# Setting a planner's durations, its rule for two shared engines and its due times anew, in a kernel of attention and two gated MLPs

## The chip, the cores and the metric

The kernel runs on one core of a Trainium2 chip. A core has five engines that run side by side: TensorE (PE, the matmuls), VectorE (DVE), ScalarE (ACT), GpSimd (POOL) and SyncE (SP), which here issues the transfers. The metric is the device time of one launch in microseconds; three runs of the kernel before gave 1060.21 us as the median (1059.39 to 1060.55).

## The reference

```python
# q, k, v: 4 batches x 8 heads x 576 positions x 64
scores = q @ k.T / 8                     # masked: heads 0-3 a window of 32 positions,
attn = softmax(masked scores)            # heads 4-7 every 4th of the last 128 positions
x = heads side by side of (attn @ v)     # 2304 tokens x 512
xn = x / sqrt(mean(x*x) + 1e-6) * rms_g
g = xn @ w_gate;  h = silu(g) * (xn @ w_val);  x = h @ w_out      # 512 -> 1536 -> 512
gate = sigmoid(x @ w_gate2)
return (gate * (x @ w_val2)) @ w_out2                             # 512 -> 1536 -> 512
```

The six weights come as 64-bit numbers and are turned into f32 on the chip.

## The kernel before, in words

**Stages.** Attention is done in 48 groups (batch, pair of heads, third of the positions). A group is a chain: S on PE (`scores`, L811), three masks with row maxima on DVE (L822), three exponentials on ACT (L828), two small DVE steps (L835, L836), three products with the reciprocal sums on POOL (L841), T on PE (transposes, L855), a copy on ACT (L859), O on PE (L867), a copy into x on ACT (L878, L886). Once enough groups of a chunk of 384 tokens are there, `x_norm` squares x on ACT (L911), adds the four parts on POOL (L919), sums over the partitions on PE (L927, called q below), finds the root on DVE and POOL (L943 to L965), spreads it (DVE L968, PE L983, called r below) and scales (L995). The first MLP then takes the chunk in steps: gate products g and value products v on PE (12 matmuls each, L1124), tanh on ACT (L1136), two products on DVE (L1138, L1142), the split of h in a high part (ACT L473) and a low part (POOL L477 or DVE L480), and one step later four output products y (L1159). There are 72 steps: two passes over half the hidden units, six chunks in each, six steps a chunk. The first dense step starts while most groups are still to do; the rest of attention is laced into the first pass. The second MLP follows in three passes by a block scheme with 7 products instead of 8 (L1361, L1280); its operands are sums of blocks (`combos` L1026/L1029, `weight_blocks` L553/L556, L595/L598), each again split in a high and a low part.

**Weights.** One of the 72 weight tiles is loaded into `wst` (L431, L435), squared on ACT (L451) and converted by four DVE instructions (L457, L460, L463, L466); then it is split (L473, L477), or, for those that are used later, stored and loaded again (`weight_ahead`, `weight_late`).

**What sets the order.** Nothing is scheduled at run time. While the program is built, every piece of work is an operation with one or several engines that may do it, a duration for each, a due time, and what it reads and writes (`Line.add`, L122). `Line.emit` (L164) walks a model clock: for each engine it takes among the operations that are ready the one that can start first, and of those the one with the earliest due time; it puts the operation at the end of that engine's instruction stream, and moves the engine's clock by its duration. So durations and due times decide which instruction stands before which on each engine, and which engine does an operation that may be done by two. On the chip each engine then runs its stream in order. The durations are numbers in `PARAMS` (L25), small functions of the elements (`act`, `dve`, `dves`, `pool`, L337 to L351) and literals in the `add` calls. `Shared` marks durations of DVE and POOL operations that slow each other (`shared`, L92). `clocked` (L108) is the model of PE's two clocks. `cross` and `same` (L233) are what passes from the end of an operation to the start of one that needs it. A penalty per kind of operation (`w_lo`, `h_lo` ...) makes the second engine less welcome. The dense matmuls keep one fixed order among themselves ("PE order"); where a group's S, T and O fall between them is the planner's choice.

Of the kernel before, what the change touches and what calls it, by code (L numbers as in the profile page):

```python
# [24 lines left out]
PARAMS = {  # L25
    "margin": 272.425, "wait": 0.781, "w_sq": 2.027, "w_hi": 0.389, "w_lo": 1.94, "x_hi": 0.358,
    "x_lo": 0.048, "h_hi": 1.944, "h_lo": 0.349, "qk": 0.226, "norm": 3.767, "pts": 4.555,
    "o": 0.012, "snap": 53.824, "h_ahead": 56.759, "h2_ahead": 11.517, "evac": 7.152,
    "holds": (6, 6), "norm_act": 0.994, "slack": 0.0, "share_v": 0.45, "share_p": 0.35,
    "cold": 1.7, "low": 0.27, "high": 0.38, "recip": 0.43, "rel1": 171.35, "span1": 76.226,  # L30
    "rel2": 16.017, "span2": -0.378, "ys": 11.771, "ts": 0.198, "cross": 0.08, "same": 0.064,
    "dma_lat": 2.0, "dma_rate": 260000.0, "by_pe": 0, "turn0": -164.047, "turn1": -260.061,
    "turn2": -126.4, "att0": -244.604, "span0": 93.904, "lo1": -2.027, "hi1": 20.942, "lo2": 3.37,
    "hi2": 50.7, "lo3": 43.938, "hi3": 64.292, "lo4": 57.9, "hi4": 101.971, "lo5": 47.17,
    "hi5": 159.918, "ld_a": -436.996, "ld_b": -493.817, "ld_v": -356.0, "ld_c": -347.0,
    "ld_d": -331.0, "lead": -12.321, "xdue": 4.486, "wdue": -7.2, "wslope": 2.65,
    "wload": -430.961, "wload_step": 37.9, "warm_n": 18, "warm_t": 10.103, "warm_dt": 0.322,
    "warm_c": 19, "warm_m": 5, "warm_late": 0.218, "warm_due": 15.435, "mask_cost": 0.335,
    "exp_cost": 0.56, "s_cost": 0.75, "o_cost": 0.6, "t_cost": 0.38, "pt_lead": 6.997,
    "x_lead": 91.83, "wy_due": -0.712, "y_from": 5.542, "y_step": 1.029, "xb_due": 1.637,  # L40
    "y_last": 0.244, "xb_last": 13.017,
# [34 lines left out]
class Line:  # L76
# [7 lines left out]
    HOLD = "DVE", "ACT", "PL"  # L84

    def __init__(self):
        self.ops, self.writer, self.readers = [], {}, {}
        self.now = self.bus = 0.0
        self.last = {}
        self.work, self.window, self.warm = 0.0, 0, True  # L90

    def shared(self, eng, start, cost, free):  # L92
# [5 lines left out]
        took = float(cost)  # L98
        if mate in self.last:
            s, e = self.last[mate]  # L100
            both = max(0.0, min(start + took * (1 + slow[eng]), e) - max(start, s))
# [145 lines left out]
def attention_then_two_gated_mlps(  # L247
# [15 lines left out]
    nc = tc.nc  # L263
# [1346 lines left out]
```

## Time and profile before

| | |
|---|---|
| median of 3 runs | 1060.21 us |
| the profiled execution | 1063.01 us, of which the span of its instructions 1061.2 us |
| PE busy | 995.7 us, 94% |
| DVE, ACT, POOL busy | 728.1 us (69%), 483.5 us (46%), 553.4 us (52%) |
| granted clock of PE, mean | 0.967 of full speed |

How to read it: matmuls are pipelined, so the time from one start to the next is the price of a matmul, not the duration that a row gives. A stretch of the span can be lost in two ways: PE waits, or it runs at the lower of its two clocks (granted clock 0.5 is 1.2 GHz, 1.0 is 2.4 GHz). "Idle before" an instruction is put down to what came last, so an arrow to POOL says that a POOL instruction ended that wait. A row's x12 counts matmul instructions; S and O of one group are 12 of them in the trace, T is 3.

### The profile page before, as it was taken

The numbers are of one execution on the slowest core, as the hardware profiler recorded it, in microseconds if no ns is written. First come the engines' busy times: TensorE is split into PE (matmuls) and PEld (weight loads), VectorE is DVE, ScalarE is ACT, GpSimd is POOL, SyncE is SP. The second block draws the span as 40 slices with busy tenths as digits, with TensorE's granted clock in tenths as the row PEclk, the third lists the DMA queues.
The fourth block names the chain that finished last, engine by engine and source line by source line (L and its number), as shares of the span: only waits on it lengthen the run. The fifth ranks groups of instructions, "written<-read, shape, count | busy, mean of one in ns | idle before, by whom it ended". The sixth has DMA issues, their size and how long they took to land. (4 is left out here: it accounts for less than half of the span.)

```text
span 1061.2 us, 20091 instructions
## 1 busy us (share of the span) xinstructions
PE 995.7 (94%) x7078; PEld 953.3 (90%) x7078; DVE 728.1 (69%) x1559; ACT 483.5 (46%) x1338; POOL 553.4 (52%) x757
## 2 busy tenths in 40 slices
PE   5889789989999989999999998998999999999997
PEld 4668678888999989999999997998999999999996
DVE  4587865667865687877773658567776567785665
ACT  3756645656333443223222445455663445544331
POOL 3457784554443572122324757457785458755432
PEclk9859989999999989999999999999999999999998
DMA  8836638675638456796885665246145564267642
GB/s 173 166 90 201 137 101 188 145 222 155 208 105 322 169 177 224 253 312 202 298 288 194 220 214 186 99 170 243 66 153 217 206 241 141 84 220 229 177 83 53
DMA packets 203653, 194.53 MB, mean 183 GB/s; under 512 B 136928, under 2 KB 166176, under 8 KB 203552
## 3 DMA queue, kind: packets, MB, share of 16 engines
q1 hardware_dynamic: 203552, 193.25, 58.6%
q8 instruction: 56, 0.92, 0.4%
q14 instruction: 45, 0.37, 0.1%
HBM read 129.50 MB, written 63.70 MB: 182 GB/s over the span
## 5 line engine op out<-in xcount | busy, mean ns | idle before, releaser
L477 POOL TENSOR_TENSOR h<-t,h 128x288 fp32r<-128x288 f32 (+1 forms) x219 | 206.7, 955 | 303.7 <-ACT h L473 285.2
L473 ACT CAST h<-t 128x288 fp32r<-128x288 f32 (+1 forms) x240 | 108.6, 457 | 175.9 <-DVE t L1142 93.5
L1124 PE MATMUL g<-xo,w 128*128 128x384 f32 x864 | 171.1, 346 | 2.3 <-ACT w L473 1.4
L1159 PE MATMUL y<-h,wo 128*128 128x384 f32 x864 | 171.3, 342 | 0.8 <-POOL h L477 0.4
L1124 PE MATMUL v<-xo,w 128*128 128x384 f32 x864 | 165.2, 339 | 4.6 <-DVE t L1142 4.6
L1280 PE MATMUL y<-h,wo 128*128 128x288 f32 x1008 | 162.1, 299 | 3.9 <-POOL h L477 1.8
L1124 PEld LDWEIGHTS g<-xo,w 128*128 128x128 f32 x864 | 156.2, 195 | 5.3 <-ACT w L473 1.5
L1124 PEld LDWEIGHTS v<-xo,w 128*128 128x128 f32 x864 | 151.7, 190 | 6.2 <-DVE t L1142 5.3
L1159 PEld LDWEIGHTS y<-h,wo 128*128 128x128 f32 x864 | 150.9, 190 | 3.1 <-POOL h L477 0.7
L1280 PEld LDWEIGHTS y<-h,wo 128*128 128x128 f32 x1008 | 143.9, 190 | 6.8 <-POOL h L477 3.4
L1239 DVE SCALAR_TENSOR_TENSOR pt<-y,pt 128x288 f32<-128x288 f32 x136 | 61.4, 452 | 61.9 <-PE y L1280 53.1
L1136 ACT ACTIVATE t<-g 128x384 f32<-128x384 f32 x72 | 35.4, 492 | 121.3 <-PE g L1124 121.2
L1138 DVE SCALAR_TENSOR_TENSOR t<-t,g 128x384 f32<-128x384 f32 x72 | 39.6, 550 | 62.3 <-ACT t L1136 62.3
L841 POOL TENSOR_SCALAR pr<-pr,rs 128x96 f32<-128x96 f32 x139 | 60.1, 449 | 39.7 <-DVE rs L836 18.8
L1377 DVE TENSOR_TENSOR t<-t,att 128x288 f32<-128x288 f32 x96 | 43.0, 448 | 39.3 <-PE att L1361 36.6
L457 DVE TENSOR_SCALAR wz<-wz 128x512 f32<-128x512 f32 x72 | 44.9, 623 | 32.1 <-ACT wz L451 31.8
L463 DVE SCALAR_TENSOR_TENSOR wz<-wst,wz 128x512 int32<-128x512 int32 x72 | 64.1, 890 | 1.4
L451 ACT ACTIVATE wz<-wst 128x512 f32<-128x512 f32 x71 | 47.5, 669 | 28.2 <-DMA wst<-in_moe_w_gate_dram 11.2
L460 DVE SCALAR_TENSOR_TENSOR wz<-wst,wz 128x512 int32<-128x512 int32 x72 | 59.0, 820 | 1.8
L466 DVE SCALAR_TENSOR_TENSOR wz<-wst,wz 128x512 int32<-128x512 int32 x72 | 59.2, 824 | 1.4
L1026 DVE TENSOR_TENSOR t<-t,t 128x288 f32<-128x288 f32 x62 | 49.3, 796 | 13.9 <-POOL h L477 13.5
L828 ACT ACTIVATE pr<-pr,nmx 128x96 f32<-128x96 f32 x144 | 52.4, 367 | 11.6 <-DVE nmx L822 11.3
(205 smaller groups left out, 1800.7 us busy)
## 6 DMA issues: line engine op xcount, KB each, us to landing
z<-wz SPq DMA_DIRECT2D x54, 256.0 KB
xo<-xs SPq DMA_DIRECT2D x23, 576.0 KB
wst<-in_moe_w_gate_dram SPq DMA_DIRECT2D x24, 512.0 KB
wst<-in_moe_w_val_dram SPq DMA_DIRECT2D x24, 512.0 KB
wst<-in_moe_w_out_dram SPq DMA_DIRECT2D x24, 512.0 KB
xs<-xs SPq DMA_DIRECT2D x21, 576.0 KB
wst<-xs SPq DMA_DIRECT2D x18, 576.0 KB
x<-xo SPq DMA_DIRECT2D x12, 768.0 KB
```

What stands on the lines that cost most here:

```text
L460: add("DVE", Shared(0.68), lambda: nc.vector.scalar_tensor_tensor(out=z.t, in0=top(), scalar=3, in1=z.t, op0=ALU.logical_shift_left, op1=A ...
L463: add("DVE", Shared(0.68), lambda: nc.vector.scalar_tensor_tensor(out=z.t, in0=top(), scalar=-0x40000000, in1=z.t, op0=ALU.bitwise_and, op ...
L466: add("DVE", Shared(0.68), lambda: nc.vector.scalar_tensor_tensor(out=z.t, in0=low(), scalar=29, in1=z.t, op0=ALU.logical_shift_right, op1 ...
L473: add("ACT", act(n), lambda: nc.scalar.copy(out=hi(), in_=src()), reads=reads, writes=[key] + [order] * bool(order), tiles=tiles + [dst], ...
L477: add("PL", pool(n), lambda: nc.gpsimd.tensor_tensor(out=lo(), in0=src(), in1=hi().bitcast(F32), op=ALU.subtract), reads=reads, writes=[ke ...
L828: add("ACT", PARAMS["exp_cost"], lambda u=u: nc.scalar.activation(out=pr.t[:, u], in_=pr.t[:, u], func=ACTF.Exp, bias=nmx.t[:, u:u + 1], s ...
L841: add("PL", Shared(0.33), lambda u=u: nc.gpsimd.tensor_scalar(out=pr.t[:, u], in0=pr.t[:, u], scalar1=rs.t[:, u:u + 1], scalar2=1.0, op0=A ...
L1026: add("DVE", dves(n), lambda: nc.vector.tensor_tensor(out=dst(), in0=a(), in1=c(), op=ALU.subtract), reads=reads, writes=writes, tiles=til ...
L1124: nc.tensor.matmul(out=bank.t, lhsT=w[:, l, cols], rhs=x[:, r, j], start=kk == 0 and n == 0, stop=kk == KD - 1 and n == 2)
L1159: nc.tensor.matmul(out=yb.t, lhsT=w.t[:, l, s], rhs=h.t[:, r], start=n == 0 and j == 0, stop=n == HOLDS[p] - 1 and j == 2)
L1239: add("DVE", dve(T), lambda: nc.vector.scalar_tensor_tensor(out=t.t[:, e, h], in0=bank.t, scalar=0.5, in1=t.t[:, e, h], op0=ALU.mult, op1= ...
L1280: nc.tensor.matmul(out=bank.t, lhsT=w.t[:, u, a, n], rhs=hs[u].t[:, d], start=first and u == 0 and m == 0, stop=u == NF // 2 - 1 and m == ...
```

## The change

Only what the planner believes changes, and the due times and penalties that were chosen with it; the operations stay the same but for one ordering key in `x_ops` (the first pass of the second MLP now shares one order of the `xo` buffers with the loads of the first). In the diff: the fixed share of the durations goes down (DVE 0.155 to 0.065, ACT 0.17 to 0.09), a latency after an operation is added for each engine (`TAIL`, `AFTER`), masks cost 0.18 instead of 0.335 and exponentials 0.36 instead of 0.56, the root on POOL 3.9 instead of 2.6, the low part on DVE a `Shared` duration instead of 0.25 + n/400; when DVE and POOL overlap, both are made longer, and what waits for the one that already runs is moved too. `margin` and `wait` now switch off the rule by which an overdue operation could go ahead of its turn. Transfers get 1.7 us and 330 GB/s instead of 2.0 us and 260 GB/s. The due times were chosen with durations scattered at random.

```diff
-    "margin": 272.425, "wait": 0.781, "w_sq": 2.027, "w_hi": 0.389, "w_lo": 1.94, "x_hi": 0.358,
+    "margin": 1670.351, "wait": 0.0, "w_sq": 7.654, "w_hi": 0.38, "w_lo": 2.585, "x_hi": 0.454,
...
+    TAIL = {"PE": 0.16, "DVE": 0.085, "ACT": 0.085, "PL": 0.035}
+    AFTER = {"PE": -0.16, "DVE": 0.034, "ACT": 0.034, "PL": 0.078}
...
-            both = max(0.0, min(start + took * (1 + slow[eng]), e) - max(start, s))
-            took += both * slow[eng]
-            if start > s:
-                free[mate] += both * slow[mate]
+            if e > start:
+                took = min(took / (1 - slow[eng]), took + slow[eng] * (e - start))
+                both = min(start + took, e) - start
+                self.longer = min(both * slow[mate] / (1 - slow[mate]),
+                                  took * slow[mate])
+                free[mate] += self.longer
+                self.last[mate] = s, e + self.longer
...
+            if self.longer:
+                mate = self.mate[{"DVE": "PL", "PL": "DVE"}[o.eng]]
+                mate.end += self.longer
...
-            o.start, o.end = start, start + cost + o.lat
+            o.start, o.end = start, start + cost + o.lat + self.TAIL.get(o.eng, 0.0)
...
-        return Shared(0.12 + n / 950)
+        return Shared(0.055 + n / 950)
...
-            other=(kind + "_lo", "DVE", 0.25 + n / 400, lambda: nc.vector.tensor_tensor(
+            other=(kind + "_lo", "DVE", dves(n), lambda: nc.vector.tensor_tensor(
...
-            add("PL", 2.6, newton_aside, writes=[yk], tiles=[a, y, ms], due=due)
+            add("PL", 3.9, newton_aside, writes=[yk], tiles=[a, y, ms], due=due)
...
-                [f"{o.ring.tag} order"] * (p == ONE and o.ring.tag != "xo"), tiles=[o],
+                ["x order" if o.ring.tag == "xo" else f"{o.ring.tag} order"] * (p == ONE), tiles=[o],
```

What that does to the order is seen at three places. Lines of the changed kernel are 16 to 19 higher (L811 is L830 there, L1124 is L1143).

SP, the first transfers of the program, before: `xo` takes the keys and queries of the first pairs of heads, `wst` a weight tile, `xT` values.

```order
L375 DMA gam_133<-in_moe_rms_g_dram 128x4x1
L649 DMA xo_209<-in_k_dram 72x16x64
L649 DMA xo_214<-in_q_dram 72x16x64
L649 DMA xo_233<-in_k_dram 72x16x64
L649 DMA xo_242<-in_q_dram 72x16x64
L431 DMA wst_254<-in_moe_w_gate_dram 128x4x256
L431 DMA wst_258<-in_moe_w_val_dram 128x4x256
L723 DMA xT_220<-in_v_dram 64x4x64
```

The same place now:

```order
L394 DMA gam_133<-in_moe_rms_g_dram 128x4x1
L450 DMA wst_209<-in_moe_w_gate_dram 128x4x256
L450 DMA wst_211<-in_moe_w_val_dram 128x4x256
L454 DMA wst_222<-in_moe_w_out_dram 128x1024
L668 DMA xo_236<-in_k_dram 72x16x64
L668 DMA xo_245<-in_q_dram 72x16x64
L668 DMA xo_256<-in_k_dram 72x16x64
L668 DMA xo_262<-in_q_dram 72x16x64
L742 DMA xT_220<-in_v_dram 64x4x64
```

Three weight tiles of 512 KB now stand ahead of the first keys and queries, where two stood behind them.

PE in the third and fourth dense step, where groups are laced in, before (L811 is S, L855 T, L867 O, L1124 g and v, L1159 y):

```order
L1124 MATMUL v<-xo,w 128x384 x12
L811 MATMUL att<-kT,qT 64x96 x6
L1159 MATMUL y_1237<-h,wo 128x384 x3
L1159 MATMUL y_1257<-h,wo 128x384 x3
L1159 MATMUL y_1262<-h,wo 128x384 x3
L855 MATMUL att<-ident,pr 96x128 x3
L1159 MATMUL y_1270<-h,wo 128x384 x3
L855 MATMUL att<-ident,pr 96x128 x3
L867 MATMUL att<-pts,v 64x64 x12
L855 MATMUL att<-ident,pr 96x128 x3
L867 MATMUL att<-pts,v 64x64 x6
L1124 MATMUL g<-xo,w 128x384 x12
```

The same place now:

```order
L1143 MATMUL g<-xo,w 128x384 x12
L886 MATMUL att<-pts,v 64x64 x6
L874 MATMUL att<-ident,pr 96x128 x3
L1143 MATMUL v<-xo,w 128x384 x12
L886 MATMUL att<-pts,v 64x64 x6
L830 MATMUL att<-kT,qT 64x96 x6
L1178 MATMUL y_1369<-h,wo 128x384 x3
L874 MATMUL att<-ident,pr 96x128 x3
L1178 MATMUL y_1380<-h,wo 128x384 x3
L1178 MATMUL y_1387<-h,wo 128x384 x3
L886 MATMUL att<-pts,v 64x64 x6
L1178 MATMUL y_1402<-h,wo 128x384 x3
```

Before, three T and O follow each other with no dense matmul between them; now there is a dense piece between each T and the O that needs it.

PE at the first sum over the partitions behind the first dense step (L927 is q, L983 r), before:

```order
L1124 MATMUL v<-xo,w 128x384 x12
L1159 MATMUL y_1237<-h,wo 128x384 x3
L1159 MATMUL y_1257<-h,wo 128x384 x3
L1159 MATMUL y_1262<-h,wo 128x384 x3
L1159 MATMUL y_1270<-h,wo 128x384 x3
L855 MATMUL att<-ident,pr 96x128 x3
L811 MATMUL att<-kT,qT 64x96 x6
L867 MATMUL att<-pts,v 64x64 x6
L927 MATMUL att<-ones,pt 128x1 x3
L855 MATMUL att<-ident,pr 96x128 x3
L1124 MATMUL g<-xo,w 128x384 x12
L867 MATMUL att<-pts,v 64x64 x6
```

The same place now:

```order
L886 MATMUL att<-pts,v 64x64 x6
L1178 MATMUL y_1369<-h,wo 128x384 x3
L1178 MATMUL y_1380<-h,wo 128x384 x3
L946 MATMUL att<-ones,pt 128x1 x3
L1178 MATMUL y_1387<-h,wo 128x384 x3
L1178 MATMUL y_1402<-h,wo 128x384 x3
L874 MATMUL att<-ident,pr 96x128 x3
L830 MATMUL att<-kT,qT 64x96 x6
L886 MATMUL att<-pts,v 64x64 x6
L830 MATMUL att<-kT,qT 64x96 x12
L1002 MATMUL att<-ident,rb 128x128 x3
L1143 MATMUL g<-xo,w 128x384 x12
```

Before, q follows an O at once, and r comes behind the 12 matmuls of g; now two y stand between O and q, and r comes before g.

Counts over the whole program: the low part of h is done by POOL 219 times and by DVE 21 times before, and 182 and 58 times now. Of the 72 weight tiles, 5 are converted on DVE ahead of the first scaling of x (L995) before, 8 now; 7, 11, 18, 33, 36, 61 and 72 of them ahead of the first DVE product (L1138) of step 1, 4, 8, 24, 28, 52 and 68 before, and 9, 13, 19, 37, 39, 72 and 72 now. At the first dense matmul 14 S, 13 T and 12 O are behind PE before, 16, 15 and 14 now; when the seven first steps are done, 26, 24 and 24 before, and 27, 25 and 24 now.

## Rows read from the trace of the kernel before

**Rows 1.** Busy time by stretch; columns: stretch and length, engines busy (instructions), granted clock, DMA, GB/s.
```profile
core 0 of [0], span 1061.2 us
0.00:21.80 21.80, 9.48 (x50) 8.49 (x50) 7.89 (x15) 6.54 (x14) 8.83 (x34) 1.00 0.83 175
21.80:43.40 21.60, 16.50 (x226) 13.58 (x225) 17.04 (x85) 16.61 (x73) 11.59 (x31) 0.99 1.00 187
43.40:69.60 26.20, 22.56 (x185) 18.56 (x185) 14.94 (x63) 16.17 (x58) 9.25 (x22) 0.50 0.49 90
69.60:157.50 87.90, 74.77 (x576) 64.89 (x577) 70.22 (x191) 54.11 (x174) 65.58 (x95) 0.86 0.56 145
157.50:420.00 262.50, 253.78 (x1845) 240.41 (x1845) 180.02 (x431) 120.17 (x353) 126.61 (x210) 0.98 0.64 190
420.00:560.00 140.00, 138.31 (x797) 137.72 (x796) 107.61 (x163) 40.24 (x75) 37.63 (x29) 1.00 0.79 271
560.00:1000.00 440.00, 426.82 (x3043) 419.02 (x3042) 294.95 (x540) 211.72 (x549) 274.21 (x315) 1.00 0.51 175
1000.00:1061.20 61.20, 53.46 (x366) 50.58 (x364) 35.38 (x75) 17.91 (x45) 19.67 (x25) 0.94 0.42 106
```
**Rows 2.** PE's waits, 69.6 to 157.5 us: total, times, longest.
```profile
PE att L927 <- POOL pt L919: 6.2, 1, 6.2
PE att L855 <- POOL pr L841: 2.3, 6, 0.6
PE g L1124 <- ACT w L473: 1.4, 1, 1.4
```
**Rows 3.** PE's waits, 157.5 to 420 us.
```profile
PE att L983 <- DVE rb L968: 4.4, 3, 2.6
PE v L1124 <- DVE t L1142: 2.9, 1, 2.9
```
**Rows 4.** Timeline of PE; columns: start, duration, instruction [idle before].
```profile
63.84 1.22 PE L811 MATMUL att<-kT,qT 64*64 64x96 f32 x12
...
85.07 0.49 PE L855 MATMUL att<-ident,pr 128*96 128x128 f32 x3
85.31 1.81 PE L1159 MATMUL y<-h,wo 128*128 128x384 f32 x9
87.06 0.71 PE L811 MATMUL att<-kT,qT 64*64 64x96 f32 x12
87.70 0.57 PE L867 MATMUL att<-pts,v 96*64 96x64 f32 x12
88.20 2.35 PE L1124 MATMUL g<-xo,w 128*128 128x384 f32 x12
...
136.01 1.44 PE L927 MATMUL att<-ones,pt 128*128 128x1 f32 x6 [6.16 <-POOL pt L919]
...
142.97 0.52 PE L983 MATMUL att<-ident,rb 128*128 128x128 f32 x3 [0.47 <-DVE rb L968]
...
152.76 2.24 PE L1124 MATMUL v<-xo,w 128*128 128x384 f32 x12
154.84 2.24 PE L1159 MATMUL y<-h,wo 128*128 128x384 f32 x12
```
**Rows 5.** DVE's longest conversion step: count, busy us, mean ns.
```profile
L463 DVE SCALAR_TENSOR_TENSOR wz<-wst,wz 128x512 int32<-128x512 int32 x72 | 64.1, 890 | 1.4
```
**Rows 6.** The same line alone, busy time in one stretch (DVE).
```profile
420.00:560.00 140.00, 24.03 (x25) 1.00 0.79 271
```
**Rows 7.** Timeline of ACT, its first work.
```profile
13.24 0.66 ACT L451 ACTIVATE wz<-wst 128x512 f32<-128x512 f32 x1 [11.24 <-DMA wst<-in_moe_w_gate_dram]
13.80 0.41 ACT L673 COPY kT<-g 128x288 f32<-128x288 f32 x1
```
**Rows 8.** Timeline of SP's queue, the first weight load.
```profile
6.75 1.82 SPq L431 DMA_DIRECT2D wst<-in_moe_w_gate_dram  x1
```
**Rows 9.** The low part of h on DVE: shortest, median, longest ns, first and last start.
```profile
L480 DVE TENSOR_TENSOR h<-t,h x21: 447/765/1533, 365.3 to 943.2; 128x288 fp32r<-128x288 f32 x14, 128x384 fp32r<-128x384 f32 x7
```

More of the change, by code (lines that the diff above doesn't have):

```diff
@@ L88, in __init__ @@
         self.now = self.bus = 0.0
-        self.last = {}
+        self.last, self.mate, self.longer = {}, {}, 0.0
         self.work, self.window, self.warm = 0.0, 0, True
@@ L212, in emit @@
             cost, fn, _ = o.ways[o.eng]
+            self.longer = 0.0
             cost = self.shared(o.eng, start, cost, free)
+            if self.longer:
+                mate = self.mate[{"DVE": "PL", "PL": "DVE"}[o.eng]]
+                mate.end += self.longer
+                for t in mate.tiles:
+                    t.freed = max(t.freed, mate.end)
+                for s in mate.succs:
+                    for e in s.ways:
+                        if s.seq in ready[e]:
+                            was = ready[e][s.seq][1]
+                            ready[e][s.seq] = s, max(was, mate.end + PARAMS["cross"])
+            if isinstance(o.ways[o.eng][0], Shared):
+                self.mate[o.eng] = o
             if o.eng == "PE":
@@ L474, in split @@
             reads=reads, writes=[key] + [order] * bool(order), tiles=tiles + [dst], due=due,
-            other=(kind + "_hi", "DVE", 0.25 + n / 600, lambda: nc.vector.tensor_copy(
+            other=(kind + "_hi", "DVE", Shared(0.06 + n / 1920), lambda: nc.vector.tensor_copy(
                 out=hi(), in_=src())))
@@ L858, in attn_group @@
             writes=[("pt", gk)], tiles=[pr, pt, pts], due=due + 1.87)
-        add("ACT", 0.48, lambda: nc.scalar.copy(out=pts.t, in_=pt.t), reads=[("pt", gk)],
+        add("ACT", 0.385, lambda: nc.scalar.copy(out=pts.t, in_=pt.t), reads=[("pt", gk)],
             writes=[("pts", gk)], tiles=[pt, pts], due=due + 2.18,
-            other=("pts", "DVE", 0.5, lambda: nc.vector.tensor_copy(out=pts.t, in_=pt.t)))
+            other=("pts", "DVE", 0.465, lambda: nc.vector.tensor_copy(out=pts.t, in_=pt.t)))
         o = bank(2, "o", [P, G * QB])
@@ L887, in put @@
                 pos += n
-        add("ACT", 0.25, lambda: put(nc.scalar.copy), reads=[("o", gk)], writes=[("x", gk)],
+        add("ACT", 0.43 if dil and g == 1 else 0.23, lambda: put(nc.scalar.copy), reads=[("o", gk)], writes=[("x", gk)],
             tiles=[o, xT[b]], due=due + 2.81,
-            other=("o", "DVE", 0.25, lambda: put(nc.vector.tensor_copy)))
+            other=("o", "DVE", 0.44 if dil and g == 1 else 0.28, lambda: put(nc.vector.tensor_copy)))
     xtile = {}
@@ L971, in x_norm @@
         if c:
-            add("DVE", 0.75, seed, reads=[("ssp", c)], writes=[yk], tiles=[ssp, ms, a, y], due=due)
-            add("PL", 2.6, newton_aside, writes=[yk], tiles=[a, y, ms], due=due)
-            add("DVE", 0.56, spread, reads=[yk], writes=[("rb", c)], tiles=[y, rb], due=due)
+            add("DVE", 0.5, seed, reads=[("ssp", c)], writes=[yk], tiles=[ssp, ms, a, y], due=due)
+            add("PL", 3.9, newton_aside, writes=[yk], tiles=[a, y, ms], due=due)
+            add("DVE", 0.47, spread, reads=[yk], writes=[("rb", c)], tiles=[y, rb], due=due)
         else:
@@ L983, in turn @@
                 nc.tensor.transpose(rbp.t[:, t], rb.t[:, t], ident)
-        add("PE", 0.36, turn, reads=[("rb", c), "ident"], writes=[("rbp", c), "x order"],
+        add("PE", 0.32, turn, reads=[("rb", c), "ident"], writes=[("rbp", c), "x order"],
             tiles=[rb, rbp] + xo, due=due)
```

58 lines of the change are left out of this document (27 added, 31 removed), and 5 rows, old and new, of the table PARAMS.

## The prediction

> **What bounds the kernel now.** I read the busy time by stretch first, then PE's waits in each stretch, then the timeline where a wait was long. PE is busy 995.7 of 1061.2 us, and from 420 us on it is the bound almost without a gap: 138.31 of 140 us, then 426.82 of 440 [rows 1]. A planner's table takes no matmul away, so all that it can move is time in which PE waits or runs at the lower clock. The stretches say where that lies: 12.3 us of waiting up to 21.8 us, 5.1 up to 43.4, 3.6 up to 69.6 (there at a granted clock of 0.50, the 1.2 GHz level, all the way), 13.1 up to 157.5 (clock 0.86), 8.7 up to 420, 1.7 up to 560, 13.2 up to 1000 and 7.7 in the end [rows 1]. 65 us in all, over half of it in the first 157.5 us, where the groups of attention hang on chains through all engines.
>
> What a step costs at the full clock: 12 value products start at 152.76 and the y behind them at 154.84, so 2.08 us, and three such pieces are a step of 6.24. Of a group, S takes 0.64 us (87.06 to 87.70), O 0.50 (to 88.20), T 0.24 (85.07 to 85.31): 1.38 us together. At the lower clock the row of S is 1.22 us and not 0.71, 1.7 times as long [rows 4].
>
> **The change, stretch by stretch.** Beside the order of instructions only their engine changes, so I price each stretch by what stands in a new place.
>
> *0 to 69.6 us, up to the first dense matmul.* Three weight tiles now go ahead of the first keys and queries. ACT did nothing before 13.24 us, when the first weight had landed (6.5 us after its issue at 6.75), and the first copy of kT stood behind that one at 13.80 [rows 7, 8]. So the keys were there and waited for ACT; they may come later by some 3 us and lose little. The bound from above: 1.57 MB at the mean 175 GB/s of that stretch [rows 1] is 9.0 us; from below it is 0, since ACT and DVE start earlier. On ACT, eight instructions for weights now stand ahead of the first copy of kT, one before. What is won is that 8 weight tiles are converted before the first scaling and not 5: four DVE instructions each, the longest 0.89 us [rows 5], so up to 10.7 us of DVE work moved into time in which DVE was idle (7.89 of 21.8 us busy [rows 1]). What is lost is that 16 S, 15 T and 14 O stand ahead of the first dense matmul and not 14, 13 and 12: two groups more, 2 x 1.38 x 1.7 = 4.7 us at the lower clock, less what falls into the 3.6 us of waits. I take +4 us for all this; bounds -6 (the lower clock comes later) and +14 (keys 9 us late, and the groups in full).
>
> *69.6 to 157.5 us, seven steps.* The old order has 41.6 us of dense work in it (seven steps, but six y), 12 S, 11 T and 12 O for 16.3, and about 1 us of q and r: 59 of 87.9 us. 28.9 us are lost, 13.1 by waiting, 15.8 by the lower clock and what goes with it. Three things change. First, 11 S, 10 T and 10 O are left, 14.4 us: -1.9. Second, the waits of T for POOL's products (2.3 us) and of g for a weight (1.4) [rows 2]: T and O followed each other with no dense matmul between, and between the fourth and the eighth step 7 tiles were converted, where it is 6 now, nearly one a step; I take half of the 3.7, -1.8. Third, q. It waited 6.2 us for POOL's additions. Now two y (1.04 us) stand between the last O and q, and POOL has only two of three additions left behind that O; but r is now ahead of g. From the end of q (136.01 + 1.44 = 137.45) to r at 142.97 the root took 5.5 us [rows 4]; the new order has two y, T, three S and an O in between, 1.04 + 0.24 + 1.92 + 0.50 = 3.7, so r waits 1.8 where it waited 0.5, and g and the whole dense chain stand behind it on PE. With some 1.4 left of q's wait, 3.2 instead of 6.6, -3.4. Each long wait is followed by matmuls at the lower clock, so with 5.2 of 13.1 us of waits gone, 5.2/13.1 of the 15.8 would go too, 6.3; clock and waits need not go together, and I take 4. The sum is -11 us; bounds -19 (two thirds of the loss go) and +3 (the waits move, and r waits for a POOL that is late).
>
> *157.5 to 560 us.* The waits are r, 4.4 us in three, and one of v, 2.9 [rows 3]. The planner now knows that the root takes longer, so r gets later places; but weights for the second MLP are all converted by step 52, not by step 68, and that loads DVE. Between steps 28 and 52 it converts 33 tiles. In the 140 us from 420 on it did 25 [rows 6], or 27 in the 150 us of 24 steps; 6 more, at up to 3.6 us, are 21 us on a DVE that is busy for 107.61 of 140 us [rows 1]: from 77% to 91%. That still hides behind PE, whose g and v have 4.16 us between the end of one use of a bank and the next. I take -2 us; bounds -7 and +6.
>
> *560 to 1000 us.* 13.2 us of waits, in many small pieces for ACT, POOL and DVE [rows 1]. Over the program DVE takes 37 more low parts of h, most of them here, from POOL, which is 274.21 of 440 us busy. I take -3 us; bounds -8 and +5.
>
> At this place the trace shows a price and a page has a rule. A low part on DVE took from 447 to 1533 ns, 765 in the median [rows 9]; the planner's new price is 0.055 + 288/950 = 0.36 us alone, and some share more while POOL works. The Trainium skill, "SBUF — State Buffer", Who interferes with whom, says that the port pair which DVE and GpSimd share is an exclusive lock, that a DVE instruction with two inputs from SBUF contends with a GpSimd one that reads SBUF, and that issue order decides who is blocked. The low part has two such inputs, and the spread of 447 to 1533 agrees with a lock rather than with a share. By the rule each of the 37 can stand still for a whole POOL instruction, and if the longest row held for all of them, 37 x (1.53 - 0.77) = 28 us would be added to DVE, not to PE: the term would shrink from -3 to about -2. I keep -3, by the median row.
>
> *1000 us to the end.* PE's last 33 rows of products and transposes have the same order; only the y before them are spread wider. 0, bounds -2 and +2.
>
> **The sum.** +4 - 11 - 2 - 3 + 0 = -12 us, on the profiled execution's 1063.0 us: 1051. That execution lies 2.8 us above the median of the three runs (1060.2), so I predict 1048 us.
>
> **The rivals.**
> - *The waits move.* Each wait that goes is replaced by the next late one, as r for q. For it: in 69.6 to 157.5 us DVE is busy 70.22, POOL 65.58 and PE 74.77 of 87.9 us, so little room is left for a better order. Against it: 10.7 us of conversions have left that stretch and the one before. It gives -2 to +2 around the median, 1058 to 1062.
> - *Slower by the start.* PE keeps the 2.4 GHz level from 21.8 to 43.4 us (0.99) though it is busy for only 16.5 of 21.6 us; from then on it is at 1.2 GHz until the dense matmuls come [rows 1]. If the keys come late, PE has less to do before 21.8 us (9.48 us busy now), and the clock can fall then and stay low up to the dense matmuls, as it did from 43.4 on. Then those 16.5 us become 28, 6.5 more than the stretch is long; with keys 3 us late, the two groups at 4.7, and -10 of what the later stretches give, it is +4, 1064 in the median's terms; without the later gains 1074. It decides from the point at which the first S starts later than about 25 us (21.8 now, where my first stretch ends). For it: eight instructions ahead of the first kT copy on ACT. Against it: that copy waited for a weight before as well.
> - *DVE becomes the bound from step 28 to 52.* At 91% by the sum above, a tenth more would make it the longest engine. If a step became 0.3 us longer for 24 steps, 7 us come back: 1055. Against it: the stretch from 420 on had no stall of note at 77%.
> - *The change does not do what it says.* The model's numbers can be nearer to the chip and the order no better, since in the stretches from 420 on there is little to win. That is the first rival's time.
>
> **How the numbers follow.** The forecast has 0.60, with a range of its own of 1036 to 1056; the waits that move 0.14; the slow start 0.20; DVE as the bound 0.06. The likeliest time is 1048 us. The range must reach into the slow start, and down to where the bounds of the first two stretches both come out well (-2 and -18 instead of +4 and -11): 1033 to 1066 us. About 0.2%, 2 us, is what a measurement here can tell from no change. Faster by more: 0.60, 0.05 of the DVE case and 0.04 of the waits that move, 0.69. Within 0.2%: 0.09, out of the waits that move. Slower: the slow start and what is left, 0.22.
>
> **What would show it.** Of the start: first S at 21 to 25 us, the first dense matmul between 68 and 76, and DVE busy for over 12 us before 21.8. Of the seven steps: they take 75 to 80 us instead of 87.9, q's wait is below 3 us and r's about 2. Of the middle: DVE at about 90% between steps 28 and 52 with PE still full, and no conversions behind step 52. Of the second MLP: PE's idle time from 560 to 1000 us falls to about 10. Wrong would be a first S behind 25 us with the clock at 0.5 from there on, a long wait for r, or PE waiting for DVE's products between 340 and 500 us.

## The result, and the profile after

The changed kernel takes 1042.82 us (median of 4, 1041.47 to 1044.65), the kernel before beside it 1060.38 (1059.39 to 1062.14): a ratio of 0.9834 [0.9812, 0.9856], 17.6 us faster. 1048 was predicted. The profiled execution has a span of 1039.7 us, 21.5 less than that of before.

First the busy time by stretch of the changed kernel, cut where the same work begins as in [rows 1] or close to it (first S, first dense matmul, step 7, second MLP, tail); the columns are those of [rows 1]:

```profile
0.00:23.70 23.70, 8.75 (x50) 7.79 (x50) 12.37 (x20) 8.35 (x17) 10.20 (x35) 0.76 0.84 199
23.70:47.40 23.70, 19.81 (x232) 15.18 (x231) 17.12 (x87) 20.42 (x84) 13.88 (x32) 0.80 0.94 183
47.40:73.70 26.30, 19.78 (x234) 16.14 (x234) 20.72 (x88) 20.75 (x78) 14.54 (x32) 0.74 0.56 117
73.70:144.20 70.50, 66.11 (x533) 58.92 (x532) 63.88 (x167) 46.98 (x152) 54.82 (x82) 0.93 0.66 167
144.20:393.80 249.60, 249.55 (x1837) 236.84 (x1837) 197.34 (x451) 125.34 (x358) 131.13 (x205) 1.00 0.73 220
393.80:534.00 140.20, 140.20 (x811) 140.12 (x810) 88.37 (x141) 40.37 (x74) 42.77 (x37) 1.00 0.74 260
595.50:977.80 382.30, 364.98 (x2670) 356.76 (x2669) 263.31 (x497) 190.88 (x501) 225.24 (x257) 1.00 0.48 167
977.80:1039.70 61.90, 54.08 (x370) 51.24 (x369) 35.37 (x78) 18.32 (x46) 18.09 (x22) 0.94 0.42 107
```

From 144.2 us to the end of the first MLP PE is busy all the time, at the full clock: where [rows 1] has 8.7 us of waiting up to 420 us and a clock of 0.98, there is nothing left to take. The lower clock before the dense matmuls is spread otherwise, 0.80 and 0.74 where it was 0.99 and 0.50. In the seven steps PE idles for 4.4 us instead of 13.1.

The same piece of work found in both PE timelines gives the shifts. The first dense matmul is 4.1 us later (69.6 and 73.7 us). Step 7 begins 13.3 us earlier (157.5, 144.2), so the seven steps gave 17.4. The dense matmuls have one order in both kernels, and the one that ran at 560.0 now runs at 531.2, another 15.5. The same 12 gate products in PE's timelines of before and after:

```profile
559.43 2.24 PE L1124 MATMUL g<-xo,w 128*128 128x384 f32 x12
```
```profile
530.64 2.24 PE L1143 MATMUL g<-xo,w 128*128 128x384 f32 x12
```

The matmul that ran at 1000.0 runs at 978.4: 7.2 are given back. The second MLP alone takes 7.7 longer, and 0.5 were won between 560 us and its start. The tail takes as long as it did. 4.1 - 17.4 - 15.5 + 7.2 + 0.1 = -21.5 us.

What is left of the waits in the seven steps: the longest of PE's waits in the changed kernel (73.7 to 144.2 us; the next is 0.6), and its timeline at q and r:

```profile
PE att L1002 <- DVE nmx L841: 3.2, 1, 3.2
```
```profile
118.39 0.72 PE L946 MATMUL att<-ones,pt 128*128 128x1 f32 x6
...
126.77 0.87 PE L1002 MATMUL att<-ident,rb 128*128 128x128 f32 x3 [3.18 <-DVE nmx L841]
127.29 4.19 PE L1143 MATMUL g<-xo,w 128*128 128x384 f32 x12
```

q does not wait at all (6.16 us in [rows 4]), nor T for POOL's products (2.3 in [rows 2]); r waits 3.2 us, and the g behind it runs for 4.19 us at a granted clock of 0.50 (127.3 to 131.3 us), where [rows 4] has 2.35.

Why the middle has no wait is seen at the root. POOL's timeline of the kernel before, the first two and the last of the root's twelve small operations ahead of the longest wait for r (221.01 us, 2.65):

```profile
216.02 0.19 POOL L961 TENSOR_TENSOR rsa<-rsy 128x3 f32<-128x3 f32 x1 [3.10 <-DVE rsy L947]
216.30 0.75 POOL L962 TENSOR_TENSOR rsa<-rsa,ms 128x3 f32<-128x3 f32 x1
...
220.08 0.20 POOL L965 TENSOR_TENSOR rsy<-rsy,rsa 128x3 f32<-128x3 f32 x1
```

The same root in the changed kernel, its first and its last operation, and PE's r after it:

```profile
209.31 0.20 POOL L980 TENSOR_TENSOR rsa<-rsy 128x3 f32<-128x3 f32 x1 [0.83 <-DVE rsy L966]
...
212.38 0.20 POOL L984 TENSOR_TENSOR rsy<-rsy,rsa 128x3 f32<-128x3 f32 x1
```
```profile
215.37 0.49 PE L1002 MATMUL att<-ident,rb 128*128 128x128 f32 x3
```

This root took 4.3 us before (216.02 to 220.28) and takes 3.3 now; 2.6 had been planned, 3.9 is now. POOL's wait for the seed on DVE fell from 3.1 to 0.8 us, and PE does 2.8 us of other work between the end of the root and r. But the roots did not become quicker: the five on POOL took 3.3 to 4.6 us before and take 3.3 to 5.0 now, 4.0 and 4.4 in the mean. What changed is r's place. In the four units behind step 7 PE had 4.6 to 6.4 us of work between q and r, and has 6.4 to 13.0 now; r's longest wait there is 0.05 us instead of 2.65.

The second MLP is the part that became slower. PE's longest waits there, before (624.8 to 999.5 us) and then after (595.5 to 977.8):

```profile
PE g L1361 <- POOL xo L477: 3.0, 2, 1.5
PE v L1361 <- ACT t L1371: 2.2, 4, 1.5
PE g L1361 <- DVE t L1377: 1.7, 2, 1.3
```
```profile
PE g L1380 <- DVE t L1396: 5.6, 6, 2.3
PE att L1380 <- DVE wst L499: 1.8, 2, 0.9
PE g L1380 <- DVE xo L499: 1.6, 2, 0.8
PE att L1380 <- DMA xo<-xs: 1.6, 2, 1.3
```

All waits together are 12.8 us before and 17.3 after, and PE's busy time there went from 361.9 to 365.0. The longest, in the changed kernel's timelines of PE and of DVE:

```profile
742.02 1.08 PE L1380 MATMUL g<-xo,w 128*128 128x288 f32 x6 [2.34 <-DVE t L1396]
```
```profile
737.90 0.92 DVE L1045 TENSOR_TENSOR t<-t,t 128x288 f32<-128x288 f32 x1
738.74 1.03 DVE L572 TENSOR_TENSOR S<-wz,S 128x256 f32<-128x256 f32 x1
739.69 1.01 DVE L572 TENSOR_TENSOR S<-wz 128x256 f32<-128x256 f32 x1
740.62 0.98 DVE L1045 TENSOR_TENSOR t<-t,t 128x288 f32<-128x288 f32 x1
741.52 0.44 DVE L1396 TENSOR_TENSOR t<-t,g 128x288 f32<-128x288 f32 x1
```

g needs the bank that DVE's addition (L1396, 0.44 us) empties, and DVE does four sums of about 1 us each first. The same sum L1045 takes 0.44 us at 737.17, where POOL is idle beside it, so beside a busy POOL this queue is about twice as long. In the 50 us behind the wait the granted clock is 0.97.

### The profile page after: what moved, and what is told of

Its sections match the earlier page's. It is cut to its first block, busy times and chain, and to the rows that moved or that the text cites. A ratio compares the mean times of both kernels' runs of the same rounds, so it can differ in the third digit from the quotient of the medians.

```text
span 1039.7 us, 20082 instructions
## 1 busy us (share of the span) xinstructions
PE 984.6 (95%) x7078; PEld 944.1 (91%) x7078; DVE 726.3 (70%) x1570; ACT 490.6 (47%) x1349; POOL 541.2 (52%) x735
## 4 chain that ended last, share of the span: by engine, by line
PE 76%; DVE 8%; DMA 5%; SPq 3%; POOL 3%; issue 2%; ACT 2%; DVEq 0%; POOLq 0%; ACTq 0%
PE g L1143 14%; PE y L1178 14%; PE v L1143 14%; PE y L1299 11%; PE att L1380 7%; PE v L1380 6%; PE g L1380 4%; PE att L830 2%; DMA xo<-xs 2%; PE att L886 1%; PE att L874 1%; DVE t L1045 1%; DVE t L1412 1%; DVE t L1396 1%; SPq L742 1%
## 5 line engine op out<-in xcount | busy, mean ns | idle before, releaser
L496 POOL TENSOR_TENSOR h<-t,h 128x288 fp32r<-128x288 f32 (+1 forms) x182 | 176.9, 980 | 292.8 <-ACT h L492 269.4
L1178 PE MATMUL y<-h,wo 128*128 128x384 f32 x864 | 168.6, 339 | 0.1
L1143 PE MATMUL g<-xo,w 128*128 128x384 f32 x864 | 166.4, 340 | 0.0
L1143 PE MATMUL v<-xo,w 128*128 128x384 f32 x864 | 162.9, 336 | 0.0
L1143 PEld LDWEIGHTS g<-xo,w 128*128 128x128 f32 x864 | 152.8, 191 | 1.3 <-issue 0.2
L1143 PEld LDWEIGHTS v<-xo,w 128*128 128x128 f32 x864 | 150.3, 188 | 0.5
L1396 DVE TENSOR_TENSOR t<-t,att 128x288 f32<-128x288 f32 x96 | 43.0, 448 | 45.8 <-PE att L1380 45.1
L479 DVE SCALAR_TENSOR_TENSOR wz<-wst,wz 128x512 int32<-128x512 int32 x72 | 62.3, 866 | 1.5
L482 DVE SCALAR_TENSOR_TENSOR wz<-wst,wz 128x512 int32<-128x512 int32 x72 | 59.7, 829 | 1.3
L485 DVE SCALAR_TENSOR_TENSOR wz<-wst,wz 128x512 int32<-128x512 int32 x72 | 58.2, 808 | 1.1
L1161 DVE TENSOR_TENSOR t<-t,v 128x384 f32<-128x384 f32 x72 | 39.6, 550 | 25.8 <-PE v L1143 25.1
L1380 PE MATMUL att<-wst,w 128*128 128x288 f32 x336 | 54.5, 296 | 2.7 <-DVE wst L499 1.8
```

The source lines that it names most:

```text
L479: add("DVE", Shared(0.595), lambda: nc.vector.scalar_tensor_tensor(out=z.t, in0=top(), scalar=3, in1=z.t, op0=ALU.logical_shift_left, op1= ...
L482: add("DVE", Shared(0.595), lambda: nc.vector.scalar_tensor_tensor(out=z.t, in0=top(), scalar=-0x40000000, in1=z.t, op0=ALU.bitwise_and, o ...
L485: add("DVE", Shared(0.595), lambda: nc.vector.scalar_tensor_tensor(out=z.t, in0=low(), scalar=29, in1=z.t, op0=ALU.logical_shift_right, op ...
L496: add("PL", pool(n), lambda: nc.gpsimd.tensor_tensor(out=lo(), in0=src(), in1=hi().bitcast(F32), op=ALU.subtract), reads=reads, writes=[ke ...
L1143: nc.tensor.matmul(out=bank.t, lhsT=w[:, l, cols], rhs=x[:, r, j], start=kk == 0 and n == 0, stop=kk == KD - 1 and n == 2)
L1178: nc.tensor.matmul(out=yb.t, lhsT=w.t[:, l, s], rhs=h.t[:, r], start=n == 0 and j == 0, stop=n == HOLDS[p] - 1 and j == 2)
```

## The experiments

The theory was that the measured durations clear the first MLP of waits (A), against due times alone (B); the second MLP's loss was put down in turn to low parts on DVE's queue (A in run 4), late operand loads (C), durations without slack (D) and DVE's choice of work (H). Each kernel was timed beside the kernel before. The stages are read from PE's timeline of one execution at the same matmuls, the second MLP from its first to the 1830th matmul record of its g, v and att; all in us, the ratio is that to the kernel before.

| kernel | ratio | first dense | step 7 | second MLP begins | second MLP takes |
|---|---|---|---|---|---|
| before | 1 | 69.6 | 157.5 | 624.8 | 374.8 |
| changed | 0.9834 [0.9812, 0.9856] | 73.7 | 144.2 | 595.5 | 382.5 |
| 1 durations alone | 0.9994 [0.9974, 1.0015] | 77.3 | 159.2 | 612.6 | 382.8 |
| 2 due times alone | 0.9891 [0.9857, 0.9926] | 70.6 | 155.0 | 611.0 | 379.3 |
| 3 before, root at 3.9 | 0.9946 [0.9917, 0.9975] | 66.2 | 157.6 | 615.8 | 375.0 |
| 4 low parts back | 0.9845 [0.9814, 0.9877] | 73.8 | 144.2 | 596.6 | 383.8 |
| 5 second MLP, old prices | 0.9951 [0.9929, 0.9972] | 77.4 | 147.9 | 600.7 | 395.0 |
| 6 first loads back | 0.9884 [0.9859, 0.9909] | 75.9 | 152.0 | 604.3 | 382.7 |
| 7 keys first | 0.9927 [0.9899, 0.9956] | 73.3 | 156.9 | 608.6 | 383.0 |
| 8 operand loads early | 0.9837 [0.9813, 0.9862] | 75.5 | 145.8 | 597.1 | 382.0 |
| 9 banks first | 0.9805 [0.9778, 0.9833] | 74.9 | 145.4 | 596.7 | 382.2 |
| 10 old sharing | 0.9925 [0.9894, 0.9955] | 71.1 | 144.0 | 600.1 | 386.4 |
| 11 root at 2.6 | 0.9983 [0.9963, 1.0003] | 74.9 | 149.9 | 613.8 | 382.2 |
| 12 two planners | 0.9795 [0.9767, 0.9823] | 73.0 | 143.1 | 596.1 | 378.8 |

Kernels 4, 5, 8, 9 and 12 have the changed kernel's order on PE all through the first MLP (on DVE, 4 and 5 leave it at 202 us, 8 and 12 at 465). The spread of these six, 73.0 to 77.4 at the first dense matmul and 595.5 to 600.7 at the end, is that of one order run again, and most of it comes from before the first dense matmul: from there to the end they take 521.5 to 523.3. At step 7, kernels 6 and 7 have 36 and 24 small matmuls of attention more behind them than the changed one (1081 and 1069 records against 1045), so the end of the first MLP is the fairer mark.

**1, 2: durations or due times.**
Kernel 1 is the changed one with every due time and penalty of the kernel before (`margin` and `wait` among them), and only those; kernel 2 is the kernel before with the changed ones. Kernel 2's edit begins:
```diff
-    "margin": 1670.351, "wait": 0.0, "w_sq": 7.654, "w_hi": 0.38, "w_lo": 2.585, "x_hi": 0.454,
+    "margin": 272.425, "wait": 0.781, "w_sq": 2.027, "w_hi": 0.389, "w_lo": 1.94, "x_hi": 0.358,
...
```


> The changed kernel's durations and sharing rules (root 3.9, masks, exponentials, transfers, shares) with the due times and penalties of the kernel before. Theory A (the measured durations remove the first MLP's waits): between a sum q and its root r stand 9.9 to 16.5 us of TensorE work in all six units of the first MLP (5.2 to 9.3 in five of six before), so no r waits over 1.5 us and no q over 3; start near 70 us as before, steps 0 to 7 in 70 to 78 us, steps 7 to the end of the first MLP in 450 to 458 us, second MLP near 375 us as before, because only 16 of 144 low parts of its h stand on VectorE (34 after, 13 before): 1030 to 1040 us. Theory B (the due times do it): the waits come back and the time is 1054 to 1061 us.

> The kernel before with the changed kernel's due times and penalties, durations and sharing rules left as they were. Theory A: the units whose root stands only 5.9 and 8.2 us of TensorE work behind its sum wait for it (3 us and 1 us), the other four (12 us or more) don't; masks and exponentials are planned too long, so steps 0 to 7 stay near 78 to 85 us, and the second MLP is as slow as after, 380 to 384 us, with 39 of 144 low parts on VectorE: 1046 to 1056 us. Theory B: all of the gain is here, 1040 to 1046 us.

At the end of the first MLP the durations alone are worth 12.2 us and the due times alone 13.8; both 29.3, a little over the sum. Neither theory holds by itself. The durations cleared the steps behind step 7 (453.4 us with 1.6 of waiting, 467.3 before), but not the steps ahead of it (159.2), and lost 8.0 in the second MLP: in the whole nothing is left. I had expected 1030 to 1040; the start, the seven steps (81.9 us) and the second MLP were all wrong. The due times alone had no r wait, though I expected 3 us at a distance of 5.9. In the seven steps PE has 5.6 us of work between q and r there, and the root begins 1.7 us behind q and takes 4.8; r does not wait because the g between them waits 4.9 us for its weight (PE's waits of kernel 2, 70.6 to 155 us):

```profile
PE g L1123 <- ACT w L472: 2.7, 1, 2.7
PE g L1123 <- POOL w L476: 2.2, 1, 2.2
```

One late piece hides the other there. Behind step 7 no r waits over 0.11 us, with 5.0 to 13.0 us of work between.

**3, 11: the root by itself.**
Kernel 3 is the kernel before with the edit below, kernel 11 the changed one with its reverse:
```diff
-            add("PL", 2.6, newton_aside, writes=[yk], tiles=[a, y, ms], due=due)
+            add("PL", 3.9, newton_aside, writes=[yk], tiles=[a, y, ms], due=due)
```


> The kernel before with one number changed: the root (Newton steps on GpSimd) planned at 3.9 us, not 2.6. Theory A: the TensorE work between sum and root goes from 6.7, 5.2, 8.7, 7.9, 9.3 and 12.4 us to 6.7, 10.3, 12.3, 9.5, 13.3 and 15.5, so the three r waits of 157.5 to 420 (4.4 us) and the r wait near 143 go; the q wait of 6.2 us stays: 4 to 9 us faster than before, 1051 to 1056 us. Theory B: within 2 us of before.

> The changed kernel with the root planned at 2.6 us again, as before the change. Between sum and root then stand 16.2, 13.3, 12.4, 8.4, 12.4 and 24.6 us of TensorE work, against 16.2, 5.2, 12.9, 10.4, 12.4 and 25.6 in the changed kernel; with 8.4 to 9 us from sum to root as measured (5.2 of work and a wait of 3.2 in the changed kernel), there is a wait of less than 1 us in the fourth unit and none in the second. Theory A2 (what decides is the distance in TensorE's order, to which due times and durations both add): no r wait over 1 us, end of the first MLP at 595 to 602 us, 1040 to 1047 us. Rival (only the root's own duration moves it): r waits of 2 to 4 us come back in three units, 1048 to 1056 us.

One number on the kernel before takes 9.0 us off the end of the first MLP, and the second keeps its 375.0. Up to 139.6 us its order on PE is that of the kernel before, so the 3.4 us between their first dense matmuls is again one order's spread. No r wait over 0.12 us is left behind step 7; the q wait of 6.1 stays, as expected. The stretch from step 7 on in kernel 3:

```profile
157.60:615.80 458.20, 452.79 (x2996) 438.15 (x2996) 314.89 (x636) 183.48 (x475) 208.72 (x279) 1.00 0.68 219
```

The clock is 1.00 there and PE idles for 5.4 us instead of 10.8; between q and r stand 6.1 to 7.8 us of work. The other way round the number is worth twice that: with 2.6 the changed kernel's first MLP ends 18.3 us later, and I had expected at most 6.5. A part of the reason is in kernel 11's PE waits (149.9 to 613.8 us) and in ACT's timeline, which says what the 4.4 us are:

```profile
PE att L1002 <- ACT pts L878: 4.4, 1, 4.4
PE att L1002 <- DVE rb L987: 2.1, 1, 2.1
```
```profile
225.89 0.66 ACT L470 ACTIVATE wz<-wst 128x512 f32<-128x512 f32 x1 [5.85 <-DMA z<-wz]
226.46 0.50 ACT L492 CAST h<-t 128x384 fp32r<-128x384 f32 x1
226.86 0.47 ACT L878 COPY pts<-att 96x384 f32<-96x384 f32 x1
```

Only the 2.1 us are the root. For the 4.4, ACT stands for 5.85 us at a conversion whose buffer is still to be stored, and the copy that frees r's bank is two places behind it. The store's issue, in the SP queue of kernel 11, stands behind 13 pieces of values:

```profile
212.91 7.84 SPq L742 DMA_DIRECT2D v<-in_v_dram  x13
...
221.30 0.50 SPq L542 DMA_DIRECT2D z<-wz  x1
```

After that wait the granted clock is 0.86 from 225 to 250 us. So a duration that is 1.3 us wrong also moved transfers and conversions; this wait is shown. Of the 4.5 us lost in the seven steps of kernel 11 only the longest waits are known, T for DVE's scaling of x (2.2) and g for a weight's low part (1.8); what brought them about is open.

**6, 7: weights ahead of the keys.**
In the changed kernel; 6 sets back all due times of the first loads and of the first weights (two of them shown first), 7 only moves two:
```diff
-    "wload": -1256.925, "wload_step": 25.495,
+    "wload": -430.961, "wload_step": 37.9,
...
-    "ld_a": -259.215, "ld_b": -450.98,
+    "ld_a": -1310.0, "ld_b": -1300.0,
```


> The changed kernel with the due times of the first loads (first keys, queries, values) and of the first twelve weight loads set back to those before: keys and queries ahead of the weights again; durations and the due times of attention stay. Theory F (the weights loaded first make the early gain): step 7 starts near 155 to 159 us as in the kernel with new durations and old due times, not at 144, with a wait of 3 to 4 us of g for its weights' high or low part: 1052 to 1058 us. Theory G (the due times of the attention units make it, and weights first only cost the start 4 us): first S near 20 us, step 7 starts at 140 to 145, 1038 to 1043 us.

> The changed kernel with only the first four key and query loads moved ahead of the three weight loads. If the +4 us of the start come from the keys behind the weights: first S at 19 to 21 us (23.7 in the changed kernel), first step near 69 to 71 (73.7), 2 to 4 us faster, 1039 to 1041 us. If the start is bound by ScalarE, VectorE or the clock: first S earlier but the first step stays at 73 to 75, and the time within 1 us of the changed kernel.

Keys first brings the first S to 21.9 us and leaves the first dense matmul at 73.3: the 1.8 us are lost again, and between the first S and the first dense matmul PE waits 6.6 us for ACT where it waited 3.3. Then it costs 13.1 us by the end of the first MLP, and the older loads altogether 8.8, both more than the 5.2 that one order spreads. Kernel 7 took 1054.6 us, and I had expected it to be no slower than the changed one. So the order with weights first carries a part of the gain, against theory G; that these loads alone make the early gain (theory F) is not shown either, since step 7 of kernel 6 begins at 152.0 and not at 155 to 159. PE's longest waits of kernel 7 (73.3 to 156.9 us) say what keys first costs:

```profile
PE v L1143 <- POOL w L496: 4.2, 1, 4.2
PE v L1143 <- DVE t L1161: 2.4, 1, 2.4
```

A weight's low part is late, which does not occur in the changed kernel. In kernel 6 there is no such wait; there T (3.2) and r (2.3) wait for DVE's masks, so its 8.8 us are not explained by weights alone.

**10: the sharing rule.**
```diff
-            if e > start:
-                took = min(took / (1 - slow[eng]), took + slow[eng] * (e - start))
...
+            both = max(0.0, min(start + took * (1 + slow[eng]), e) - max(start, s))
+            took += both * slow[eng]
```


> The changed kernel with the rule of sharing of the kernel before (the second of two overlapping operations is made longer and the first one is not moved), all durations and due times as changed. If the new rule carries a part of the gain: it should show as waits behind VectorE and GpSimd in the first MLP, its end later by 5 to 15 us than 595.5, and 1048 to 1058 us. If the durations alone carry it (distances from sum to root 10.9 us and more in every unit): the first MLP ends at 595 to 600 us and the time is 1041 to 1047.

The first MLP ends at 600.1 us, inside the spread of the changed order, but only because the first dense matmul came at 71.1. From there to the end of the first MLP kernel 10 takes 529.0 us against the 521.5 to 523.3 of one order, so the rule is worth 6 to 7 us there, and 3.9 in the second MLP, which takes 386.4. PE's longest wait there in kernel 10 (600.1 to 987.2 us):

```profile
PE g L1376 <- DVE t L1392: 9.1, 8, 2.4
```

**4, 8, 9: which wait makes the second MLP slower.**
In the changed kernel, one edit each, in this order:
```diff
-    "h_lo": 0.114,
+    "h_lo": 0.349,
...
-    "x_lead": 13.961,
+    "x_lead": 91.83,
...
-                    writes=[ck[name]], tiles=[bank, t], due=at)
+                    writes=[ck[name]], tiles=[bank, t], due=at - 40)
```


> The changed kernel with one penalty set back (of a low part of h on VectorE, 0.349 for 0.114): 18 instead of 34 of the 144 low parts of the second MLP's h stand on VectorE; all up to the end of the first MLP is in the same order. Theory A (VectorE's queue, made longer by low parts, holds the banks that g and att wait for): the 7.6 us that g, v and att wait behind VectorE in the second MLP fall to 2 to 4, the second MLP takes 375 to 379 us, and the kernel is 3 to 7 us faster than the changed one. Theory C (the later operand loads, lead 14 for 92 us, cost it): within 1 us of the changed kernel, the same waits.

> The changed kernel with the second MLP's operand loads due 92 us ahead again, not 14. Theory C: the waits of att and g for operands that were just loaded (2.9 us in the second MLP) go and what follows is earlier, 2 to 4 us faster than the changed kernel. Theory D (planned lengths without slack): these waits go but the ones behind VectorE and ScalarE stay; at most 2 us faster.

> The changed kernel with one due time in the second MLP: VectorE's additions out of a bank (line 1396) due 40 us earlier, so that they are chosen before the sums for weights and operands (lines 572, 1045), low parts (499) and products (1412) that are ready with them. The changed kernel waits 7.5 us in the second MLP for such additions, 2.3 of them at 742 us, where VectorE first does four sums of about 1 us each. Theory H (VectorE's queue holds the banks because the wrong work is chosen first): these waits fall to 2 to 4 us, the second MLP takes 376 to 380 us, 2 to 6 us faster than the changed kernel. Rival (VectorE is full there, and what is put off is waited for next, as when the low parts were moved): the second MLP stays at 381 to 385, within 2 us.

All three leave it about where it was: 383.8, 382.0 and 382.2 us, where the changed kernel has 382.5. With the low parts back on POOL, g waits 4.5 us for ACT's high part of h instead. With the banks first, the waits behind line 1396 fall from 7.5 to 4.5, and what had been put ahead is put behind. PE's waits of kernel 9 (596.7 to 978.6 us):

```profile
PE g L1380 <- DVE xo L499: 3.1, 2, 1.6
PE g L1380 <- DVE t L1396: 2.7, 4, 1.1
PE att L1380 <- DMA xo<-xs: 2.2, 2, 1.8
```

The wait of 2.34 at 742 us is gone, that for the operand's low part has doubled, and transfers are waited for 4.9 us instead of 2.9. Theories A and H fall as causes of the whole: each wait is real, and taking it away makes another one. For theory C less is shown: with the earlier loads the waits for transfers stay, 2.6 us instead of 2.9, so the lead of the loads isn't what makes them, and what would follow if they went was not seen.

**5, 12: the old planner for the second MLP.**
Kernel 5 prices all work added for the second MLP as before and sets three of its due times and the penalty of the low part back; kernel 12 sets back all of them, and from 576 us of its plan on also latencies and the sharing rule (lines of kernel 12):
```diff
-        return 0.065 + n / 960
+        return 0.155 + n / 960 if OLD else 0.065 + n / 960
...
+            if start > 576.0 and not self.late:
+                self.late = True
...
+                PARAMS.update(BEFORE)
+                self.TAIL = {}
```


> The changed kernel, but from the start of the second MLP its VectorE, ScalarE and GpSimd operations are planned with the longer durations of the kernel before, and with its four due times there (banks emptied 53.8 us ahead, operand loads 91.8, low part 0.349, h 11.5). All up to there is unchanged. Theory D (durations planned longer than they run are a slack that covers the second MLP's scatter; with measured ones every late release is felt): the second MLP takes 373 to 377 us as before, not 382, the 17 us of waits fall to 12 or 13, and the kernel is 5 to 9 us faster than the changed one. Rival (the second MLP is slower because it is entered with other work left over on VectorE and GpSimd): it stays at 380 to 385 us.

> The changed kernel, but from the start of the second MLP the whole planner is that of the kernel before: its durations, latencies, sharing rule, penalties and due times together (the earlier attempt put back only prices and four due times). TensorE's order is the changed kernel's for all of the first MLP and the first 47 rows of the second. If the second MLP's loss comes from the planner's new numbers taken as a set: it takes 374 to 378 us as in the kernel before, its waits 12 to 14 us, and the kernel 1034 to 1039 us, 5 to 8 us faster than the changed one. If it comes from how the second MLP is entered: 381 to 386 us again and no gain over the changed kernel.

Old prices under the new latencies made the second MLP 395.0 us, the worst of all: longer durations are no slack that helps, and theory D falls. The whole old planner gave 378.8 with 13.8 us of waiting, between the two cases that I had expected: 3.7 of the 7.7 us came back. To the last of these matmuls it is less, 2.2 of 7.6 (416.8 us, 419.0 in the changed kernel, 411.4 before). One wait of 3.9 us, of g for DVE's addition, which before has not, is most of what is left (PE's waits of kernel 12, 596.1 to 974.2 us):

```profile
PE g L1428 <- DVE t L1444: 4.4, 2, 3.9
```

Kernel 12 has with 9 the lowest time of the study, but its interval overlaps that of the changed kernel, so that it beats it isn't shown. When the second MLP is entered doesn't matter: kernels 6, 7 and 11 enter it at 604 to 614 us, and it takes 382.2 to 383.0 as in the changed one. What is left over on the queues at its start was not tested: kernel 12 enters it in the changed kernel's order on PE, and stays 4.0 us above before.

## Why the prediction was right in the sum, and where it was wrong

*The bound.* That only waits and the lower clock could be won, and mostly in the first 157.5 us, was half right. PE's idle time went from 65.5 to 55.1 us of the span; the other 11.1 of the 21.5 us are busy time for the same 7078 matmul records, most of it the clock: PE was busy for 57 us at the lower level before and for 43 now, and half of that difference is 7 us. But the stretch up to 560 us gave nearly as much as the seven steps.

*0 to 69.6 us, +4.* It was +4.1. The copy of kT came 2.3 us later (16.08 us) and the first S at 23.7, as the sum had it; DVE was busy for 11.0 us up to 21.8, where I had asked for over 12. That the size fits is luck: it is no larger than the spread of this stretch, 73.0 to 77.4 us in one order, and 66.2 in kernel 3 against 69.6 in the kernel before. The two groups were priced all at the lower clock, and from the first S to the first dense matmul the clock is 0.77 in the mean. The slow start came only in its first half: the clock did fall ahead of the first S (0.50 from 16 to 23.7 us), but it did not stay there, 0.76, 0.80 and 0.74 in the three stretches.

*69.6 to 157.5 us, -11; it was -17.4.* The direction of each part was right and the size too small. I left q 1.4 us of its wait and it has none; r waits 3.2 where I had 1.8; of T's and g's 3.7 I took half and all of it went. So 8.7 us of waits went where I had 5.2. Of the lower clock I took a quarter (4 of 15.8); behind 8.7 of waits and 1.9 of work 6.8 us are left of the 17.4 (0.93 against 0.86), more than the 6.3 that I had worked out and then cut to 4.

*157.5 to 560 us, -2; it was -15.5.* This is the step that failed. "That loads DVE" was right: 33 tiles are converted between steps 28 and 52, and DVE is busy for 127.42 of those 150 us, 85% against the 91% I reckoned:

```profile
316.00:466.00 150.00, 150.00 (x867) 150.00 (x867) 127.42 (x193) 57.07 (x113) 60.34 (x53) 1.00 0.79 271
```

PE waits for none of it. I set a load of DVE against the 7.3 us of waits in [rows 3] although I had written that it hides behind PE; all of them went, as the new places of r said, and the clock, 0.98 up to 420 us, with them. PE's idle time gave 10.3 us, and the rest, 5.1, is the clock, for which I had no term here. The root's price alone gave 9.0 us there in kernel 3.

*560 to 1000 us, -3; it was +7.2.* Wrong in sign. I let DVE take the low parts and priced what POOL is spared, not that DVE's queue holds the banks. That the low parts themselves are at fault was a wrong guess of mine too (kernel 4). In the second MLP DVE does 41 of them now where it did 14, but each takes less (DVE's groups by shape, 595.5 to 977.8 us):

```profile
L499 DVE TENSOR_TENSOR h<-t,h 128x288 fp32r<-128x288 f32 x41 | 28.8, 705 | 2.8 <-ACT h L492 2.3
```

705 ns against 851 in the mean for that shape before, so the stall by the lock of which I spoke did not get worse. Which of the planner's numbers makes the 7.7 us is open; runs 4, 8 and 9 exclude three single ones, runs 1 and 2 show that the durations alone (8.0) and the due times alone (4.5) each cost something, and with all of them set back run 12 returns only about half.

*1000 us to the end, 0.* It was 0.1. The errors of two middle terms, -13.5 and +10.2, and the -6.4 of the seven steps left the sum 9.5 us short on the profiled execution. That two errors of over 10 us have opposite signs is luck, and the time would have come out much further from 1048 without it. The lower end of the range was a slip too: -2 and -18 in place of +4 and -11 give 1035, not 1033.

## What to carry to other kernels

A planner's durations and its due times are one set: here each half was worth 12 to 14 us in the first MLP, but one number put back into the whole (the root, 1.3 us) cost 18, and the second MLP got worse under every new half. Where PE is nearly full, count a removed wait with the clock behind it (here 10.3 us of waits brought 15.5), and don't discount it for an engine that gets busier but stays hidden. In a stretch whose waits are many and small on queues that run in order, taking one away shows the next: time the whole stretch, not the wait.

## What the runs showed of the hardware that was not expected

The time up to the first dense matmul varies by 4.4 us in one order (73.0 to 77.4 in the changed kernel, 4, 5, 8, 9 and 12), with a clock between 0.63 and 0.77 from the first S on; kernel 11, of the same order up to there, has 74.9 and 0.82. What follows repeats far better (from step 7 to the second MLP 451.3 to 453.0 us in the same six).

The tail ran in 59.4 us at a clock of 1.00 in kernel 9 and in 61.9 at 0.94 in the changed one, with 370 matmul records in both.

One root operation of 128x3, 0.19 us alone, took 0.75 and the next 0.64 us in the root shown of the kernel before, and at most 0.20 in that of the changed kernel: 1.0 us of the root's 4.3. DVE's timeline of the kernel before shows what ran beside them:

```profile
216.31 0.68 DVE L463 SCALAR_TENSOR_TENSOR wz<-wst,wz 128x512 int32<-128x512 int32 x1
217.03 0.69 DVE L466 SCALAR_TENSOR_TENSOR wz<-wst,wz 128x512 int32<-128x512 int32 x1
```

The two slow operations end at 217.05 and 217.78, within 0.1 us of the ends of these two conversions (216.99 and 217.72), which read two tiles. Beside the next DVE instruction (L1142, 217.64 to 218.19), one of whose inputs is the bank v, POOL's operations take 0.19 again. That the conversions hold them up is a reading of these rows, not a test.
